# Retention with two mixtures of experts on Trainium2: when the first combinations of tokens run, where the output rows are stored from, and how staged weights are spread

## The chip, the cores and the metric

One NeuronCore of one Trainium2 chip runs the whole program. The metric is device time in microseconds (us); the kernel's time is the median of several executions. The engines are TensorE (PE), VectorE (DVE), ScalarE (ACT), GpSimd (POOL), and SyncE (SP), which here only issues transfers. POOL issues transfers too.

## The reference

Three stages follow one another. Retention, for 4 batches, 8 heads, 576 positions and a head of 64, is attention without softmax, weighted by a decay. Its output, 2304 tokens of width 512, goes into a mixture of 4 experts with given weights, and that into a mixture of 8 experts of which each token uses one.

```
ret = (q k^T / 8) * gamma^(i-j), for i >= j;   x = ret v          # 2304 x 512
p = domain_probs / sum(domain_probs)
out1 = sum over e of p[:, e] * (relu(x w1[e]) w2[e])               # 4 experts, 512 -> 1024 -> 512
e* = argmax(out1 w_gate);  g = softmax(out1 w_gate)[e*];  s = sigmoid(out1 w_output_gate)[e*]
out2 = g * s * (relu(out1 w1s[e*]) w2s[e*])                        # 8 experts, one per token
```

## The kernel before

**Numbers in two parts.** Every fp32 operand of a matmul is split into a high and a low fp16 part (`split`, L163: ACT writes the high part at L164, DVE the low one at L165), and each product is three matmuls.

**Retention** goes in 24 steps of 96 positions. `at_load` (SP) brings q, k and v, `at_split` and `at_a` make scores and the running state (its new value `sn` is made by DVE at L240 and by POOL at L241), and `at_b` (L247) the step's tokens: fp32 `xf`, and their two fp16 parts in the block tile `xc` (ACT L282, POOL L283). `at_store` (L286, SP) writes `xf` to the DRAM tensor `xfd` and finished blocks to `xcd`. Four steps make a block of 384 tokens; there are 6 blocks.

**Mixture 1.** The first expert (e = 0) is interleaved with retention: the loop of L1039 walks experts e, blocks b and units u, and for e = 0 calls `at_hook` (L980), which does one retention step, four times per block. A block of e = 0 has 8 units of the first layer (`l1_first`, matmuls at L431) and three of the second (`l2`, matmuls at L534). Experts 1 to 3 do the first layer by seven products of combinations in place of eight (`l1_mixed`, matmuls at L460), 14 units: m1, m5, m6, m2, m7, m3, m4, each for two halves j. Each of m2, m7, m3 and m4 ends in a `keep` (ACT L418, DVE L419), which stores the hidden layer. m1 ends in a copy on ACT (L484), m6 in an addition on DVE (L494). Three units of `l2` follow, which DVE adds into `acc` (L546).

**Combinations of tokens.** Experts 1 to 3 need sums and differences of token parts, which are the same for each expert. For block b, `x_load` (L296) brings the plain parts from `xcd` into a tile `xc` and, the first time, four pieces of `xfd` into two tiles `xm` (L308). `x_mix` (L312) makes four differences per tile on POOL (L316), `x_keep` (L318) splits the result on ACT (L323) and DVE (L324) into `xc`, and after the second tile POOL stores it to `xcd` for later experts. For block 0 this stands in the last block of e = 0: the load at u = 0 on SP's queue (L1064), the two `x_mix` at u = 3 and 4 (L1071), the two `x_keep` at u = 8 and 9. For the other blocks it stands in e = 1, with the load on POOL's queue.

**Weights of mixture 1.** `w_load` brings eight parts of 512 KB per expert; `w_mixed` (L359) turns them into steps, in which POOL mixes quarters (L372) and ACT and DVE split them. `w_hook` (L1008) does one step. The steps of e = 1 begin in the last block of e = 0.

**Staged weights of mixture 2.** They have to lie in DRAM as two parts, `w1d` and `w2d`, before mixture 2 begins: 64 pieces of 512 KB. `s_hook` (L1015) at its i-th call loads piece i on SP (`s_load`, L556 or L559), issues the store of the split before on SP (L1023), and splits piece i - 2 (`s_split`, L562) into a tile `s16`, of which there are two. Calls stand in the loop at fixed units (L1084):

```python
if e and u in {1: (2, 8, 14) if b else (), 2: (0, 4, 8, 12), 3: (0, 3, 6, 9, 12)}[e]:
    s_hook()
```

**Shared tiles.** The tiles of `w_load`, `s_load` and `xm` come from one pool with tag "wr" and six buffers of 4 KB per partition (L132). The two `xc` buffers are shared by retention's blocks and `x_load`.

**Routing.** In e = 3 each finished `l2` unit puts closures on a list, `gate`, and each unit pops one: `g1` (transpose on PE, L597, split into `xs`), `g2` (gate logits, L608), and per block `g3` (L612), a chain of short DVE operations that ends with the store of three tiles of output rows, 774 KB, to `x1d` on SP's queue (L669). After block 4 `go_early` picks first tokens, whose rows are gathered from `x1d` by POOL (`m_x`, L850). Mixture 2 then works through slots of 128 gathered tokens.

**What sets the order.** Each engine executes its instructions in one order. The framework's planner makes it: it walks the program with times of its own, and an instruction whose operands and buffers it believes ready can move ahead of one that was written earlier. `with tc.issue_after(ins)` adds an edge: what the block writes on the engine of `ins` comes behind `ins`. The dictionary `pace` holds the last `keep` ("act", "dve") and the last weight mix ("pool"), so that splits of staged weights come behind the last `keep` written before them. In e = 1 to 3 no `keep` stands in the `l2` units nor in units 0 to 5, so hooks there hang on the last `keep` of the block before.

Of the kernel before, what the change touches and what calls it, by code (L numbers as in the profile page):

```python
# [104 lines left out]
def kernel(  # L105
# [23 lines left out]
    ht_p = ctx.enter_context(tc.tile_pool(name="ht", bufs=4, side="right"))  # L129
    x_ctx = ExitStack()  # L130
    x_p = x_ctx.enter_context(tc.tile_pool(name="x", bufs=2, side="right"))
    raw_p = ctx.enter_context(tc.tile_pool(name="raw", bufs=6))  # L132
    dram = ctx.enter_context(tc.tile_pool(name="dram", bufs=1, space=DRAM))
    ps = ctx.enter_context(tc.tile_pool(name="ps", bufs=2, space=PSUM))
    w_a = ctx.enter_context(tc.tile_pool(name="w_a", bufs=1))
# [111 lines left out]
    def at_b(s):  # L247
        x2, v2, k2 = spl.pop(s)
        p2 = pm.pop(s)
        c = s % NC  # L250
        o = ps_1.tile([128, KD, C], F32, tag="xo", name="xo")


        def into(r, p, lhsT, rhs, n, last):
            pe.matmul(  # L255
                o[64 * r:64 * r + 64, p], lhsT=lhsT, rhs=rhs,
                start=(p == 0 and n == 0), stop=last, skip_group_check=True,
            )

        for p in range(KD):  # L260
            for n, (x, y) in enumerate(TERMS):
                for r in range(2):
                    into(r, p, v2[:, x, 2 * p + r], p2[:, y, r, p], n, not c and n == 2)
        if c:
            ss = st[s - 1][1]
            for p in range(KD):
                for n, (x, y) in enumerate(TERMS):
                    for r in range(2):
                        row = slice(64 * r, 64 * r + 64)
                        into(r, p, ss[row, x, p], x2[row, y, 0, p], 3 + n, n == 2)  # L270
        st.pop(s - 1, None)
        xf = at_1.tile([128, 2, 2, C], F32, name="xf", bufs=3)
        dve.tensor_tensor(
            out=xf, in0=o.rearrange("p (a k) t -> p a k t", a=2),
            in1=cst("xtab", KD, C).rearrange("p (a k) t -> p a k t", a=2), op=ALU.mult,
        )
        b, r = divmod(s, 4)
        if r == 0:
            xcs[b] = x_p.tile([128, 2, 8, 2, HB], F16, tag="xc", name="xc")
        c, t = 2 * (r // 2), slice(C * (r % 2), C * (r % 2) + C)  # L280
        hi, lo = xcs[b][:, 0, c:c + 2, :, t], xcs[b][:, 1, c:c + 2, :, t]
        act.activation(out=hi, in_=xf, func=ACTF.Copy)  # L282
        pool.tensor_tensor(out=lo, in0=xf, in1=hi, op=ALU.subtract)  # L283
        xfs[s] = xf

    def at_store(s):  # L286
        if s < 0:
            return
        sp.dma_start(out=xfd[s * 128:(s + 1) * 128].rearrange("p (a k) t -> p a k t", a=2), in_=xfs.pop(s))
        b, r = divmod(s, 4)  # L290
        if r == 3:
            dst = xcd[b * 128:(b + 1) * 128]
            sp.dma_start(out=dst[:, :, 0:2], in_=xcs[b][:, :, 0:2])
            sp.dma_start(out=dst[:, :, 3], in_=xcs[b][:, :, 3])

    def x_load(b, mixed, q):  # L296
        t = x_p.tile([128, 2, 8, 2, HB], F16, tag="xc", name="xc")
# [264 lines left out]
    def s_split(i):  # L562
        e, j = divmod(i, 8)
        r = stage.pop(i)
        t = later["pool"].tile([128, 2048], F16, tag="s16", name="s16", bufs=2)
        if j < KD:
            w_parts(r, t.rearrange("p (a f) -> p a f", a=2), None)
            dst = w1d[e * 128:(e + 1) * 128, j].rearrange("p a f -> p (a f)")
        else:
            k = 2 * (j - KD)  # L570
            w_parts(r, t.rearrange("p (k a d) -> p k a d", k=2, a=2), True)
            dst = w2d[e * 128:(e + 1) * 128, k:k + 2].rearrange("p k a d -> p (k a d)")
        return dst, t
# [38 lines left out]
    def g3(b, pl):  # L612
# [53 lines left out]
        dve.scalar_tensor_tensor(  # L666
            out=acc[:, tb, DM], in0=iv[:, 0], scalar=SO2, in1=iv[:, 1], op0=ALU.mult, op1=ALU.mult
        )
        sp.dma_start(out=x1d[t0 * 128:(t0 + TB) * 128].rearrange("(t p) c -> p t c", p=128), in_=acc[:, tb])  # L669

    def unpermute(pl, rr, tiles, n, name):

# [366 lines left out]
    for e in range(E1):  # L1039
        for b in range(NB):  # L1040
            if e == 0:
                units = [] if b == 0 else [lambda b=b, f=f: l1_first(b, f) for f in range(KF)]
                n1 = KF
            else:
                units = l1_mixed(e, b)
                n1 = len(units)
            if (e, b) == (E1 - 1, 0):
                w3_ctx.close()
                open_routing()
            for u in range(n1 + TB):  # L1050
                if u >= n1:
                    l2(e, b, u - n1)
                    if e == E1 - 1:
                        t = b * TB + u - n1
                        gate.append(lambda t=t: g1(t, later["pool"]))
                        gate.append(lambda t=t: g2(t))
                        if u == n1 + TB - 1:
                            gate.append(lambda b=b: g3(b, later["pool"]))
                            if b == NB - 2:
                                gate.append(go_early)  # L1060
                elif units:
                    units[u]()
                if (e, b, u) == (0, NB - 1, 0):
                    x_load(0, False, sp)  # L1064
                if e and u == (2 if (e, b) == (1, 0) else 0) and (e, b) != (E1 - 1, NB - 1):
                    with tc.issue_after(pace["pool"].ins):
                        x_load((b + 1) % NB, e > 1 or b == NB - 1, pool)
                if (e, b) in [(0, NB - 1)] + [(1, i) for i in range(NB - 1)]:
                    for i in range(2):
                        if u == (3 if e == 0 else 6) + i:  # L1070
                            x_mix((b + 1) % NB, i)  # L1071
                        if u == (8, 9)[i] if e == 0 else u == (10, 12)[i]:
                            with tc.issue_after(pace["act"].ins), tc.issue_after(pace["dve"].ins):
                                x_keep((b + 1) % NB, i)
                if e == 0 and u in (2, 5, 8, 9):
                    at_hook()
                if e == 0 and nxt[0] >= NSTEP and b == NB - 1:
                    for _ in range(1 if u < n1 else 3):
                        w_hook(1)
                if e == 1 and b == 0:  # L1080
                    w_hook(1)
                if e and e + 1 < E1 and b >= 1 and u % 3 == 1:
                    w_hook(e + 1)
                if e and u in {1: (2, 8, 14) if b else (), 2: (0, 4, 8, 12), 3: (0, 3, 6, 9, 12)}[e]:  # L1084
                    s_hook()
                if e == E1 - 1:
                    if gate:
                        gate.pop(0)()
                    if b == NB - 1 and u == n1 - 1:
                        while s_at[0] <= n_stage + 2 or pend_store:  # L1090
                            s_hook()
                        m_open()
                        for s in range(EARLY):
                            m_x(s, early[5], s, TE * 128)
# [105 lines left out]
```

## Time and profile before

| | us |
|---|---|
| median of three executions | 1099.57 |
| lowest and highest | 1096.93 and 1101.28 |
| the profiled execution | 1100.34 |
| its span, first to last instruction | 1098.6 |
| PE busy in the span | 1038.0 |
| DVE, ACT, POOL busy | 539.1, 413.6, 283.1 |

The mean granted clock of TensorE is 0.983 of full speed. A busy share is a mean over stages, so the stages have to be read one by one. By the timeline, retention with the first expert takes the first 299 us, experts 1 to 3 of the first mixture end near 866 us, and the second mixture fills the rest. In a timeline row the first number is the start, the second the length, both in us; a row can merge neighbours of one group (x7); what stands in brackets is the idle time of that engine before it and what ended it. A row of busy time by stretch has the stretch, its length, then busy us (and instructions) of PE, weight loads, DVE, ACT and POOL, the granted clock, the DMA share and GB/s.

### The profile page before, as it was taken

To read this page: it belongs to the slowest core of one execution; us is meant where nothing else is said; L and a number is where in the kernel's file an instruction comes from. 1 tells how busy PE (TensorE), PEld (TensorE's weight loads), DVE (VectorE), ACT (ScalarE), POOL (GpSimd) and SP (SyncE) were. 2 spreads that over 40 slices of the span, in tenths; PEclk is the share of its full clock that TensorE was granted. 3 is DMA by queue.
4 is the path that set the end of the run, shared out by engine and by line. 5 is a ranking of instruction groups with operands and counts; after the bars stand their busy time and mean duration, and the time that the engine had idled before them with its cause. 6 is when DMAs were issued, how large, how long until landed. Compare 5 with 4: busy or idle time off the path is not lost.

```text
span 1098.6 us, 24411 instructions
## 1 busy us (share of the span) xinstructions
PE 1038.0 (94%) x10355; PEld 716.1 (65%) x10355; DVE 539.1 (49%) x1037; ACT 413.6 (38%) x821; POOL 283.1 (26%) x292
## 2 busy tenths in 40 slices
PE   4797989999999999999999999988999999999996
PEld 3664555655567777777766666765677577777774
DVE  6873665663836655544655555643665512121211
ACT  5542544542624444333434443432442112121211
POOL 5664555542544442000220000000000021212121
PEclk9898999999999999999999999999999999999998
DMA  9474324301444545655566666546623352491693
GB/s 300 150 216 120 109 89 136 95 31 59 159 154 137 207 172 211 254 195 187 200 223 243 242 242 243 168 156 219 251 107 128 133 217 75 174 356 48 224 385 132
DMA packets 52465, 196.26 MB, mean 179 GB/s; under 512 B 6510, under 2 KB 14334, under 8 KB 50048
## 3 DMA queue, kind: packets, MB, share of 16 engines
q1 hardware_dynamic: 42736, 155.47, 40.1%
q0 software_dynamic: 9616, 39.18, 10.6%
q8 instruction: 83, 1.36, 0.5%
q14 instruction: 30, 0.25, 0.1%
HBM read 184.76 MB, written 56.53 MB: 220 GB/s over the span
## 4 chain that ended last, share of the span: by engine, by line
PE 56%; DMA 16%; issue 11%; DVE 9%; POOL 4%; ACT 2%; POOLq 0%; SPq 0%; DVEq 0%; ACTq 0%
PE po L534 27%; DMA out_dram<-y_s,sidxm 8%; PE ph L460 8%; PE ph L431 7%; PE pq L460 5%; PE py L460 4%; DMA w1d<-s 3%; DVE s L165 2%; DMA wr<-in_w_dram 2%; DVE ht L419 2%; DMA out_dram<-y_s,sidxe 1%; PE xo L255 1%; POOL v L206 1%; POOL vs L199 1%; DMA w2d<-s 1%
## 5 line engine op out<-in xcount | busy, mean ns | idle before, releaser
L534 PE MATMUL po<-w,ht 128*128 128x512 f16 x1728 | 387.3, 383 | 1.3 <-DVE ht L419 1.0
L534 PEld LDWEIGHTS <-ht 128*128 128x128 f16 x1728 | 168.5, 99 | 200.6 <-issue 6.7
L460 PEld LDWEIGHTS <-w 128*128 128x128 f16 x3024 | 249.3, 98 | 4.5
L165 DVE SCALAR_TENSOR_TENSOR s<-sr,s 128x512 f16<-128x512 f32 x128 | 88.6, 730 | 65.8 <-ACT s L164 65.8
L431 PE MATMUL ph<-xc,w 128*128 128x384 f16 (+1 forms) x672 | 104.7, 314 | 17.1 <-ACT xc L282 5.8
L460 PE MATMUL ph<-xc,w 128*128 128x192 f16 x1296 | 119.4, 246 | 0.0
L875 PEld LDWEIGHTS <-lane 128*128 128x128 f16 x1920 | 109.0, 98 | 5.2 <-issue 1.1
L875 PE MATMUL p_h<-x_s,lane 128*128 128x128 f16 x1920 | 111.4, 219 | 0.6 <-issue 0.6
L164 ACT ACTIVATE s<-sr 128x512 f16<-128x512 f32 x128 | 73.4, 625 | 93.1 <-DMA w2d<-s 39.0
L892 PE MATMUL p_y<-lane,h_s 128*128 128x512 f16 x480 | 107.2, 379 | 0.8 <-DVE h_s L885 0.8
L885 DVE SCALAR_TENSOR_TENSOR h_s<-p_h,h_s 128x512 f16<-128x512 f32 x40 | 27.6, 691 | 159.2 <-ACT h_s L884 159.2
L431 PEld LDWEIGHTS <-w 128*128 128x128 f16 x672 | 65.0, 102 | 52.6 <-issue 21.0
L299 POOL DMA_DIRECT2D xc<-xcd x17 | 12.5, 736 | 295.1 <-PE py L460 295.1
L546 DVE SCALAR_TENSOR_TENSOR acc<-po,p_sb,acc 128x512 f32<-128x512 f32 x54 | 40.3, 747 | 97.2 <-PE po L534 97.2
L892 PEld LDWEIGHTS <-h_s 128*128 128x128 f16 x480 | 46.7, 98 | 52.6 <-DVE h_s L885 1.0
L460 PE MATMUL pq<-xc,w 128*128 128x192 f16 x864 | 79.7, 246 | 0.0
L460 PE MATMUL py<-xc,w 128*128 128x192 f16 x864 | 77.2, 246 | 0.0
L165 DVE SCALAR_TENSOR_TENSOR w<-wr,w 128x512 f16<-128x512 f32 x82 | 64.8, 811 | 0.8 <-ACT w L164 0.8
L372 POOL TENSOR_TENSOR wr<-wr 128x512 f32<-128x512 f32 x24 | 36.5, 1523 | 96.3 <-DVE w L165 93.4
L484 ACT ACTIVATE py<-ph 128x384 f32<-128x384 f32 x36 | 17.2, 477 | 107.5 <-PE ph L460 107.1
L895 POOL DMA_INDIRECT out_dram<-y_s,sidxm x17 | 17.3, 1019 | 145.8 <-ACT y_s L894 137.2
L884 ACT ACTIVATE h_s<-p_h 128x512 f16<-128x512 f32 x40 | 23.9, 597 | 79.4 <-PE p_h L875 75.3
(167 smaller groups left out, 1115.4 us busy)
## 6 DMA issues: line engine op xcount, KB each, us to landing
lane<-w1d SPq DMA_DIRECT2D x20, 2048.0 KB
lane<-w2d SPq DMA_DIRECT2D x20, 2048.0 KB
wr<-in_w_dram SPq DMA_DIRECT2D x32, 512.0 KB
sr<-in_w1s_dram SPq DMA_DIRECT2D x32, 512.0 KB
w1d<-s SPq DMA_DIRECT2D x32, 512.0 KB
sr<-in_w2s_dram SPq DMA_DIRECT2D x32, 512.0 KB
w2d<-s SPq DMA_DIRECT2D x32, 512.0 KB
xc<-xcd POOLq DMA_DIRECT2D x12, 960.0 KB, 9.0
```

The lines of the kernel that those rows point to most:

```text
L164: act.activation(out=hi, in_=raw, func=ACTF.Copy, scale=scale)
L165: dve.scalar_tensor_tensor(out=lo, in0=raw, scalar=scale, in1=hi, op0=ALU.mult, op1=ALU.subtract)
L372: pace["pool"] = pool.tensor_tensor(out=quarter(k, to), in0=quarter(k, x), in1=quarter(k, y), op=op)
L419: pace["dve"] = dve.scalar_tensor_tensor(out=dst[1], in0=src, scalar=0.0, in1=dst[0], op0=ALU.max, op1=ALU.subtract)
L431: pe.matmul(ph[:, h0:h1], lhsT=w[:, k, u, f * 128:(f + 1) * 128], rhs=x[:, v, k // 2 + 2 * h0:k // 2 + 2 * h1 - 1:2, k % 2], start=(n == 0 ...
L460: pe.matmul(bank[:, i], lhsT=w[:, k, u, f:f + 128], rhs=x[:, v, d, k], start=(first and i == 0 and n == 0), stop=(n == 5), skip_group_chec ...
L534: pe.matmul(po, lhsT=hts[k // 2][:, x, k % 2, i * 128:(i + 1) * 128], rhs=w[:, k, y], start=(n == 0), stop=(n == 3 * KF - 1),)
L546: dve.scalar_tensor_tensor(out=a, in0=po, scalar=p_sb[:, t, e:e + 1], in1=a, op0=ALU.mult, op1=ALU.add)
L875: pe.matmul(ph[:, j], lhsT=w[:, k, x, f * 128:(f + 1) * 128], rhs=xs[:, y, k], start=(n == 0), stop=(n == 3 * KD - 1),)
L884: act.activation(out=hi, in_=ph, func=ACTF.Relu)
L885: dve.scalar_tensor_tensor(out=lo, in0=ph, scalar=0.0, in1=hi, op0=ALU.max, op1=ALU.subtract)
L892: pe.matmul(po, lhsT=h[:, a, k], rhs=w[:, k, b], start=(n == 0), stop=(n == 3 * KF - 1))
```

## The change

The first `x_load` is tied behind the last retention store on SP, and `x_mix` behind the last POOL work written before it (in retention that is now `at_b`'s subtraction). The store of output rows moves from SP's queue to POOL's. `s16` has three buffers, the shared pool of raw tiles five. Hooks of staged weights: five per block in e = 2 and four in e = 3, where it was four and five; their number stays the same.

```diff
-    raw_p = ctx.enter_context(tc.tile_pool(name="raw", bufs=6))
+    raw_p = ctx.enter_context(tc.tile_pool(name="raw", bufs=5))
...
-        pool.tensor_tensor(out=lo, in0=xf, in1=hi, op=ALU.subtract)
+        pace["pool"] = pool.tensor_tensor(out=lo, in0=xf, in1=hi, op=ALU.subtract)
...
-            sp.dma_start(out=dst[:, :, 3], in_=xcs[b][:, :, 3])
+            pace["sp"] = sp.dma_start(out=dst[:, :, 3], in_=xcs[b][:, :, 3])
...
-        t = later["pool"].tile([128, 2048], F16, tag="s16", name="s16", bufs=2)
+        t = later["pool"].tile([128, 2048], F16, tag="s16", name="s16", bufs=3)
...
-        sp.dma_start(out=x1d[t0 * 128:(t0 + TB) * 128].rearrange("(t p) c -> p t c", p=128), in_=acc[:, tb])
+        pool.dma_start(out=x1d[t0 * 128:(t0 + TB) * 128].rearrange("(t p) c -> p t c", p=128), in_=acc[:, tb])
...
                 if (e, b, u) == (0, NB - 1, 0):
-                    x_load(0, False, sp)
+                    with tc.issue_after(pace["sp"].ins):
+                        x_load(0, False, sp)
...
                         if u == (3 if e == 0 else 6) + i:
-                            x_mix((b + 1) % NB, i)
+                            with tc.issue_after(pace["pool"].ins):
+                                x_mix((b + 1) % NB, i)
...
-                if e and u in {1: (2, 8, 14) if b else (), 2: (0, 4, 8, 12), 3: (0, 3, 6, 9, 12)}[e]:
+                if e and u in {1: (2, 8, 14) if b else (), 2: (0, 3, 7, 10, 14), 3: (0, 4, 8, 12)}[e]:
```

## Rows read from the trace of the kernel before

**Rows 1.** What PE waited for over the whole span (engine, line, releaser: us in total, times, longest)
```profile
PE pg L608 <- DVE xs L165: 9.8, 4, 3.6
```

**Rows 2.** Timeline of POOL, 80 to 100 us (start us, us, instruction, idle before it and releaser)
```profile
88.68 4.47 POOL L316 TENSOR_TENSOR xm<-xm 128x192 f32<-128x192 f32 x7 [4.62 <-DMA xm<-xfd]
...
93.11 0.61 POOL L241 TENSOR_TENSOR sn<-sn,ka 128x256 f32<-128x256 f32 x1
```

**Rows 3.** Timeline of DVE, 80 to 100 us
```profile
84.61 0.41 DVE L240 TENSOR_TENSOR sn<-u,sn 128x256 f32<-128x256 f32 x1
```

**Rows 4.** Timeline of PE, 85 to 110 us
```profile
95.88 0.41 PE L431 MATMUL ph<-xc,w 128*128 128x384 f16 x1 [5.32 <-ACT xc L282]
...
99.14 7.64 PE L431 MATMUL ph<-xc,w 128*128 128x384 f16 x35 [2.84 <-POOL xc L283]
```

**Rows 5.** Chain that ended last, in order of time (start us, us, what)
```profile
143.62 5.85 PE ph L431 x35
```

**Rows 6.** Busy time by stretch: the first five blocks of the last expert of MoE 1
```profile
672.70:709.30 36.60, 34.36 (x292) 23.43 (x291) 19.19 (x55) 13.45 (x29) 1.44 (x2) 0.95 0.56 195
709.30:747.60 38.30, 34.30 (x292) 23.52 (x291) 19.46 (x56) 13.44 (x29) 1.44 (x2) 0.96 0.55 196
747.60:785.00 37.40, 34.29 (x292) 23.39 (x291) 18.91 (x55) 13.26 (x29) 1.44 (x2) 0.95 0.57 200
785.00:820.10 35.10, 32.66 (x292) 22.98 (x291) 20.48 (x57) 13.63 (x30) 0.00 (x0) 1.00 0.47 181
820.10:853.70 33.60, 33.07 (x307) 23.38 (x306) 16.94 (x71) 9.92 (x21) 3.13 (x3) 1.00 0.39 149
```

**Rows 7.** Timeline of ACT, 700 to 720 us
```profile
707.72 1.15 ACT L164 ACTIVATE s<-sr 128x512 f16<-128x512 f32 x2 [1.93 <-DMA w2d<-s]
...
717.23 1.15 ACT L164 ACTIVATE s<-sr 128x512 f16<-128x512 f32 x2 [8.36 <-DMA w2d<-s]
```

**Rows 8.** Timeline of SP's queue, 695 to 720 us
```profile
704.55 0.34 SPq L1023 DMA_DIRECT2D w2d<-s  x1
...
706.69 0.34 SPq L1023 DMA_DIRECT2D w2d<-s  x1
```

**Rows 9.** What SP's queue waited for over the span
```profile
SPq L669 <- DVE ri L643: 84.6, 5, 21.2
```

**Rows 10.** Timeline of POOL, 770 to 890 us
```profile
780.28 0.72 POOL L299 DMA_DIRECT2D xc<-xcd  x1 [35.99 <-PE py L460]
...
880.15 1.00 POOL L851 DMA_INDIRECT x_g<-x1d,gidxm  x1 [26.94 <-DVE sidxm L685]
```

**Rows 11.** Timeline of SP's queue, 860 to 890 us
```profile
872.29 0.39 SPq L669 DMA_DIRECT2D x1d<-acc  x1
```

**Rows 12.** The page's part 6, DMA issues (KB each, median us to landing)
```profile
xc<-xcd POOLq DMA_DIRECT2D x12, 960.0 KB, 9.0
```

**Rows 13.** Groups of instructions by line and form, 270 to 300 us
```profile
L165 DVE SCALAR_TENSOR_TENSOR w<-wr,w 128x512 f16<-128x512 f32 x22 | 19.4, 919 | 0.4 <-ACT w L164 0.4
...
L372 POOL TENSOR_TENSOR wr<-wr 128x512 f32<-128x512 f32 x8 | 12.3, 1536 | 15.4 <-DVE w L165 15.0
...
L324 DVE TENSOR_TENSOR xc<-xm,xc 128x768 f16<-128x768 f32 x2 | 3.0, 1487 | 0.0
```

**Rows 14.** The page's part 5, costliest groups over the span
```profile
L165 DVE SCALAR_TENSOR_TENSOR s<-sr,s 128x512 f16<-128x512 f32 x128 | 88.6, 730 | 65.8 <-ACT s L164 65.8
```

**Rows 15.** Timeline of DVE, 300 to 306 us
```profile
304.19 0.57 DVE L494 TENSOR_TENSOR pq<-ph,s 128x384 f32<-128x384 f32 x1 [4.11 <-PE ph L460]
```

**Rows 16.** Timeline of SP's queue, 262 to 300 us
```profile
281.22 12.15 SPq L348 DMA_DIRECT2D wr<-in_w_dram  x4
```

**Rows 17.** Timeline of PE, 300 to 306 us
```profile
300.97 2.14 PE L460 MATMUL pq<-xc,w 128*128 128x192 f16 x24
```

**Rows 18.** Timeline of ACT, 580 to 600 us
```profile
596.04 0.47 ACT L484 ACTIVATE py<-ph 128x384 f32<-128x384 f32 x1 [3.12 <-PE ph L460]
```

**Rows 19.** Busy time by stretch: third expert of MoE 1
```profile
475.00:652.00 177.00, 176.87 (x1443) 125.37 (x1442) 98.12 (x163) 74.50 (x154) 21.14 (x20) 1.00 0.60 214
```

## The prediction

> **What bounds the kernel now.** I read four views in this order. The page's busy times come first: TensorE (PE) is the bound engine nearly everywhere. Then busy time by stretch: in the third expert of the first mixture PE is busy 176.87 of 177.00 us [rows 19], so nothing can be gained there, only lost. Two stretches are left in which PE waits: retention, and the last expert of the first mixture. Then the list of what PE waited for, then the timelines of the engines that it waited for.
>
> In **retention** POOL is at fault. The first combinations (x_mix of block 0, written in the last block of expert 0) have been moved forward to 88.68 us. POOL sits 4.62 us until their tiles land and runs seven of them, 4.47 us; only then, at 93.11, comes the state step sn that retention needs [rows 2]. Its operand was ready when DVE ended at 84.61 + 0.41 = 85.02 [rows 3]. What hangs on sn comes as late: PE waits 5.32 us, does one matmul, waits 2.84 us more, and does its next 35 matmuls in 7.64 us [rows 4], where the same 35 take 5.85 us elsewhere [rows 5].
>
> In the **last expert** each of four junctions between blocks is stretched. The block-to-block times are 36.60, 38.30, 37.40 and 35.10 us; the fifth junction has no staging left and takes 33.60, with 15 more matmuls [rows 6]. PE waits in four places, 9.8 us in all, for xs, the split of the routing transpose [rows 1], and the granted clock of three of these stretches is 0.95 to 0.96 against 1.00 [rows 6]. xs is late because ACT, in order, is stuck ahead of it: a staged split waits 8.36 us, up to 717.23, for the store that must empty its buffer s16 [rows 7]. That store was issued at 706.69 [rows 8], so it took about 10.5 us; the store issued at 704.55 [rows 8] had landed when the split at 707.72 began [rows 7], after 3.1 us. Three splits hang on the block's last keep and its neighbours, and two buffers make the third of them wait for a slow store.
>
> **The change, part by part.** The sum is made against the profiled execution, 1100.34 us (span 1098.6), which lies 0.8 above the median of the three runs, 1099.57.
>
> *Combinations behind the last retention step.* Out of retention go four tile loads and the two direct loads on SP, POOL's 4.62 us of waiting and eight combinations (seven in 4.47 us, so 0.64 each, 5.1 in all) [rows 2]. sn could start at 85.02 instead of 93.11, 8.1 us earlier, and the eighth combination, behind sn, leaves the chain too: 8.7 us. PE's two waits are 5.32 + 2.84 = 8.16 [rows 4], so both are covered. The slow matmuls give back 7.64 - 5.85 = 1.79. Term: -9.95. Bounds: 0, if another late operand stands at the same place, and -9.95.
>
> In their new place SP's six loads follow the last retention store, where SP has nothing more until 281.22 [rows 16]. With five raw tiles instead of six, four of them held by expert 1's parts, the second pair of combinations has to wait for a freed tile. Today's weight loads show when tiles come free: four issues from 281.22 to 293.37 [rows 16]. From there come 4.62 of landing [rows 2], four combinations, 2.6, the DVE half of x_keep, 1.49 [rows 13], and as much again at most for ACT's half: ready at 291.4 to 303.6. The first product that reads combinations starts at 300.97 [rows 17]. Bounds: 0, and 2.6 late plus a slow stretch of 1.79 as in retention, 4.4. I take 0, since tiles come free in the order in which they were filled, which is the early end.
>
> The eight combinations now also run beside DVE's weight splits. Here 22 splits took 19.4 us beside 12.3 us of POOL mixes [rows 13]; at the 0.73 of a staged split [rows 14] they would take 16.1. So 3.3 was lost to 12.3 of POOL, 0.27 per us, and 5.1 us of combinations cost DVE 1.4. DVE sits idle 4.11 us before 304.19 [rows 15], which covers that: 0. The Trainium skill (SBUF — State Buffer, section SBUF: two separate sides) has GpSimd and a two-input VectorE instruction hold one port pair exclusively, the loser blocked for the whole instruction. By that DVE would lose all 5.1 us, 1.0 past its cover, and the sum would be 1.0 higher; the row shows about a quarter of that loss.
>
> *Third s16 buffer and new hooks.* In the last expert four splits per block replace five; the third of a junction takes the buffer whose store is the early one, as the 3.1 us store was [rows 7, 8], and needn't wait. Without the wait a junction is 33.60 less the PE time of its extra matmuls, 33.07 - 32.66 = 0.41 [rows 6]: 33.19. The four sum to 147.40 [rows 6], so the term is 147.40 - 4 x 33.19 = -14.64. Bounds: 0 (the wait stays), and -14.64.
>
> The third expert takes five splits instead of four per block. ACT sits idle 3.12 us before its first due copy of the next block [rows 18], after its junction's splits; that is the cover, and no transpose or xs stands in a junction there. Bounds 0 and rival D; I take 0.
>
> *Five raw tiles* mean one load fewer ahead of the splits. No row shows a split waiting for its own load. Nearest: 960 KB landed in 9.0 us [rows 12], so 512 KB in an estimated 4.8, less the 3.12 of cover [rows 18] is 1.7 at a junction. Bounds 0 and five junctions of the second expert, 8.4 (three loaders share the tiles only there); I take one, +1.7. At the start one weight load moves behind a split: 0, covered by the part's late use in the second layer, 4.8 if not.
>
> *Output rows' store on POOL.* SP's queue waits 84.6 us for the routing at five of these stores [rows 9], with staged stores and loads queued behind; the move frees them, which is part of the term above. On POOL the six stores wait instead. An issue like this is 0.72 us, and POOL idles 35.99 before the block load [rows 10]; a load for the block after next stands behind, with a block to spare. The last store goes out at 872.29 [rows 11]; landing in 9.0 as POOL's large loads do [rows 12], it would hold the gather at 880.15 [rows 10] to 881.3. Bounds 0 and 1.1; I take 0. The Trainium skill (DMA: Bandwidth & Descriptors, section Issuing engine by pattern) gives plain stores to Sync, and its section Issuing engines are not separate DMA queues says another queue saves only issue time. By that the move wins nothing, and this sum doesn't change; the rows show what the page leaves out, a wait at the head of the queue [rows 9].
>
> Sum: -9.95 - 14.64 + 1.7 = -22.9, so 1077.4. I forecast **1077.5**.
>
> **The rivals.**
> A. The transfers, not the buffers, are late. For: the store of 10.5 us against one of 3.1 [rows 7, 8]. Then the last expert keeps its waits: 1100.34 - 9.95 + 1.7 = 1092.1.
> B. Retention gains nothing, because PE meets another late operand at once: 1100.34 - 14.64 + 1.7 = 1087.4. Against: sn alone held ACT, POOL and PE.
> C. The second combinations come late into expert 1: 1077.4 + 4.4 = 1081.8.
> D. Slower: the stall moves into the third expert. With five splits per block, two of which must get their loads inside the junction, the last split ends late and ACT's first copy of the next block with it. It decides once that split ends over 3.12 us later than now [rows 18]. At the price of the worst junction now, 38.30 - 33.19 = 5.11, six junctions cost 30.7: 1077.4 + 30.7 = 1108.1. Against: PE lost 0.13 us there [rows 19].
> E. It doesn't do what it says: the planner, with ties and buffers changed, puts other work at the same places: about 1100.
>
> **How the numbers follow.** A measurement of this kernel can tell about 0.5%, 5.5 us, from no change. Forecast 0.58 (its own range 1073 to 1083), A 0.10, B 0.08, C 0.06: all are faster by more than that, 0.82. E, and mixtures that end within 5.5 us: 0.10. D: 0.08. The range runs from 1070 (the unknown costs at 0 and some 5 us of replanned order) to 1094, past A; it leaves out D, E and 0.02 below.
>
> **What would show it.** Right: no combination on POOL before the last retention step, PE without the waits near 90 to 99 us; junctions of the last expert near 33.2 us at clock 1.00, no ACT wait over 2 us for a staged store there; x1d on POOL's queue with none of SP's 84.6 us left; the third expert still at 177 us. Wrong: PE waiting for xc in retention for another cause, for xs still, or for py copies in the second or third expert, or at 300.97 for combinations.

## The result and the profile after

The changed kernel takes 1084.3 us (median of four executions, 1082.55 to 1084.66) against 1100.25 for the kernel before beside it (1096.93 to 1101.28): a ratio of 0.9857, 95% interval 0.9833 to 0.9881. The forecast was 1077.5, the range 1070 to 1094. It got faster, as forecast, by 15.9 us in the profiled executions (1100.34 to 1084.43, spans 1098.6 to 1082.7) in place of 22.9.

To see where, I cut both spans at PE's own marks in the timeline: the first matmul of the first expert's last block (the end of retention), the first l2 matmul (L534) of a block in experts 1 to 3, the first matmul of the second mixture, the last matmul.

| stretch | before | after | difference | forecast |
|---|---|---|---|---|
| start to the end of retention | 267.52 | 258.03 | -9.49 | -9.95 |
| from there to the second expert's first l2 ("boundary") | 45.33 | 49.11 | +3.78 | 0 |
| second expert, to the third's first l2 | 177.96 | 177.98 | +0.02 | +1.7 |
| third expert, to the last's first l2 | 176.70 | 181.11 | +4.41 | 0 |
| last expert, four junctions | 147.38 | 131.09 | -16.29 | -14.64 |
| fifth junction and the way to the second mixture | 51.64 | 51.64 | 0 | 0 |
| second mixture, to the last matmul | 223.58 | 223.45 | -0.13 | 0 |
| last matmul to the end of the span | 8.49 | 10.29 | +1.80 | 0 |
| sum | 1098.6 | 1082.7 | -15.9 | -22.9 |

Both gains came, and three small losses stood where the forecast had 0. PE's timeline of the changed kernel shows one gain and two of the losses:

```profile
90.62 0.33 PE L431 MATMUL ph<-xc,w 128*128 128x384 f16 x1
91.43 5.85 PE L431 MATMUL ph<-xc,w 128*128 128x384 f16 x35 [0.49 <-POOL xc L283]
...
286.61 5.34 PE L534 MATMUL po<-w,ht 128*128 128x512 f16 x24 [2.46 <-ACT acc L544]
...
297.25 2.14 PE L460 MATMUL ph<-xc,w 128*128 128x192 f16 x24 [1.01 <-ACT py L484]
...
514.52 1.89 PE L534 MATMUL po<-w,ht 128*128 128x512 f16 x8
517.60 2.76 PE L534 MATMUL po<-w,ht 128*128 128x512 f16 x12 [1.18 <-DVE ht L419]
```

The first two rows answer to [rows 4]: the waits of 5.32 and 2.84 us are 0 and 0.49, and 35 matmuls are back at 5.85; at their end the changed kernel is 9.50 us ahead. The next two are new waits at the boundary, the last one is a new wait in the third expert. POOL's timeline of the changed kernel answers to [rows 2]:

```profile
85.32 0.86 POOL L241 TENSOR_TENSOR sn<-sn,ka 128x256 f32<-128x256 f32 x1 [1.22 <-DVE sn L240]
...
268.18 2.96 POOL L372 TENSOR_TENSOR wr<-wr 128x512 f32<-128x512 f32 x2
274.84 3.85 POOL L316 TENSOR_TENSOR xm<-xm 128x192 f32<-128x192 f32 x4 [3.71 <-DMA xm<-xfd]
278.66 6.66 POOL L372 TENSOR_TENSOR wr<-wr 128x512 f32<-128x512 f32 x4
...
514.42 3.32 POOL L372 TENSOR_TENSOR wr<-wr 128x512 f32<-128x512 f32 x2 [27.38 <-DVE w L165]
```

sn runs at 85.32 in place of 93.11, and the combinations stand behind retention. **Boundary.** The second four of them wait 3.71 us for their tile, and four weight mixes stand behind them. SP's queue says why the tile lands late, and ACT what hangs on that:

```profile
257.02 15.52 SPq L308 DMA_DIRECT2D xm<-xfd  x4
273.64 13.22 SPq L348 DMA_DIRECT2D wr<-in_w_dram  x4
```

```profile
285.36 0.63 ACT L164 ACTIVATE w<-wr 128x512 f16<-128x512 f32 x1 [1.30 <-POOL wr L372]
285.89 0.67 ACT L544 ACTIVATE acc<-po,p_sb 128x512 f32<-128x512 f32 x1
...
294.51 1.15 ACT L164 ACTIVATE w<-wr 128x512 f16<-128x512 f32 x2 [4.83 <-DMA wr<-in_w_dram]
295.57 1.25 ACT L544 ACTIVATE acc<-po,p_sb 128x512 f32<-128x512 f32 x2
```

Four `xm` loads take SP from 257.02 to 272.54, since the last two wait for a raw tile; the last weight load goes out near 286.9. ACT, in order, has weight splits ahead of its copies of the first expert's output (L544): the first copy stands behind a split that waits for POOL's late mixes, the other two behind a split that waits 4.83 us for the last weight part. PE has two `po` buffers and waits for the copies. In the kernel before PE waits nowhere in this stretch, and the same copies stand here:

```profile
292.76 0.67 ACT L544 ACTIVATE acc<-po,p_sb 128x512 f32<-128x512 f32 x1
299.19 1.25 ACT L544 ACTIVATE acc<-po,p_sb 128x512 f32<-128x512 f32 x2
```

Counted from the end of retention, the first copy comes 2.6 us later than before and the other two 5.9.

**Last expert.** Busy time by stretch over its first five blocks, answering to [rows 6]:

```profile
666.23:699.00 32.77, 32.51 (x293) 22.98 (x291) 18.58 (x54) 12.52 (x28) 2.22 (x3) 1.00 0.57 195
699.00:731.77 32.77, 32.52 (x293) 22.96 (x291) 18.58 (x54) 12.52 (x28) 2.23 (x3) 1.00 0.54 195
731.77:764.54 32.77, 32.51 (x293) 22.95 (x291) 18.57 (x54) 12.52 (x28) 2.22 (x3) 1.00 0.54 196
764.54:797.32 32.78, 32.53 (x294) 22.97 (x291) 18.57 (x54) 12.53 (x28) 2.22 (x3) 1.00 0.46 163
797.32:830.90 33.58, 33.05 (x307) 23.34 (x306) 18.74 (x76) 10.86 (x24) 0.77 (x1) 1.00 0.28 99
```

All four junctions are even, at full clock. The wait of [rows 1] is gone. Of the 16.29 us, PE's busy time gave back 135.61 [rows 6] less 130.07, 5.5: matmuls that had run at the lower granted clock. The rest was waiting. One stretch of the kernel before, right behind PE's wait of 3.6 us, shows matmuls at a granted clock of 0.50, which is 1.2 GHz in place of 2.4:

```profile
720.70:724.00 3.30, 3.30 (x12) 1.36 (x10) 0.00 (x0) 0.28 (x1) 0.00 (x0) 0.50 0.74 237
```

**Third expert.** PE's waits in this expert in the changed kernel (us in total, times, longest); the same view of the kernel before lists none:

```profile
PE po L534 <- DVE ht L419: 2.8, 4, 1.2
PE po L534 <- ACT ht L418: 0.7, 1, 0.7
```

DVE's timeline, first at the junction where PE waited 1.18, then at another:

```profile
514.25 2.36 DVE L165 SCALAR_TENSOR_TENSOR s<-sr,s 128x512 f16<-128x512 f32 x2
516.53 0.55 DVE L419 SCALAR_TENSOR_TENSOR ht<-pq,ht 128x384 f16<-128x384 f32 x1
...
545.39 1.28 DVE L165 SCALAR_TENSOR_TENSOR s<-sr,s 128x512 f16<-128x512 f32 x2
```

A staged split stands ahead of a keep whose hidden layer the l2 unit needs, and POOL's mixes at 514.42 stretch it from 1.28 to 2.36. The Trainium skill (SBUF — State Buffer, section SBUF: two separate sides) has the loser of a shared port pair blocked for the other's whole instruction. By that a split would wait, by an estimate from the row, up to 1.66 us, half of POOL's 3.32. The trace agrees in kind: the two splits lost 1.08.

### The profile page after: what moved, and what is told of

It reads as the page before. It is cut to its first block, busy times and chain, and to the rows that moved or that the text cites. A ratio compares the mean times of both kernels' runs of the same rounds, so it can differ in the third digit from the quotient of the medians.

```text
span 1082.7 us, 24429 instructions
## 1 busy us (share of the span) xinstructions
PE 1032.4 (95%) x10355; PEld 713.8 (66%) x10355; DVE 536.4 (50%) x1037; ACT 414.5 (38%) x821; POOL 289.3 (27%) x298
## 4 chain that ended last, share of the span: by engine, by line
PE 45%; issue 11%; DMA 10%; DVE 6%; ACT 1%; POOL 0%; POOLq 0%; SPq 0%; DVEq 0%; ACTq 0%
PE po L534 25%; DMA out_dram<-y_s,sidxm 8%; PE ph L460 8%; PE pq L460 5%; PE py L460 5%; DVE ht L419 2%; DVE s L165 1%; DMA out_dram<-y_s,sidxe 1%; PE tp L597 1%; PE pg L608 1%; DMA w2d<-s 0%; DVE s L505 0%; DVE w L165 0%; PE p_y L892 0%; ACT ht L418 0%
## 5 line engine op out<-in xcount | busy, mean ns | idle before, releaser
L534 PE MATMUL po<-w,ht 128*128 128x512 f16 x1728 | 384.4, 380 | 7.5 <-DVE ht L419 3.9
L534 PEld LDWEIGHTS <-ht 128*128 128x128 f16 x1728 | 167.2, 98 | 205.3 <-DVE ht L419 7.9
L165 DVE SCALAR_TENSOR_TENSOR w<-wr,w 128x512 f16<-128x512 f32 x82 | 61.7, 767 | 10.7 <-ACT w L164 10.6
L164 ACT ACTIVATE w<-wr 128x512 f16<-128x512 f32 x82 | 49.3, 623 | 19.1 <-DMA wr<-in_w_dram 13.0
L895 POOL DMA_INDIRECT out_dram<-y_s,sidxm x17 | 17.3, 1017 | 146.8 <-ACT y_s L894 138.2
```

Of the source, the lines that this page charges most:

```text
L164: act.activation(out=hi, in_=raw, func=ACTF.Copy, scale=scale)
L165: dve.scalar_tensor_tensor(out=lo, in0=raw, scalar=scale, in1=hi, op0=ALU.mult, op1=ALU.subtract)
L534: pe.matmul(po, lhsT=hts[k // 2][:, x, k % 2, i * 128:(i + 1) * 128], rhs=w[:, k, y], start=(n == 0), stop=(n == 3 * KF - 1),)
L895: pool.indirect_dma_start(out=out, out_offset=bass.IndirectOffsetOnAxis(ap=idx[:, s:s + 1], axis=0), in_=y, in_offset=None, bounds_check=N ...
```

## The experiments

Twelve kernels ran in three groups, e1 to e4, e5 to e8 and e9 to e12, once each but for e10 and e12, which ran five times. The totals of a group stand beside its own runs of the kernel before (1098.96, 1095.61 and 1098.59 us). Stretches are compared across groups, since those that an edit doesn't touch agree within 0.2 us, but for three: retention with the ties ended between 256.72 and 259.77 (the changed kernel at 258.03 and 258.39), the boundary with five raw tiles in its first order took between 48.07 and 49.75, and the second mixture, not in the table, took 223.4 to 223.9 us in the result's pair and the first group and 222.7 in the other two. So a single total says little here, and the stretches carry the argument. The last column runs from the start of the program's last store of results (POOL, L895; not the store of output rows to `x1d`) to the end of the span.

| kernel | total | retention ends | boundary | second | third | last, four | last store to end |
|---|---|---|---|---|---|---|---|
| before | | 267.52 | 45.33 | 177.96 | 176.70 | 147.38 | 7.4 |
| changed | 1084.3 | 258.03 | 49.11 | 177.98 | 181.11 | 131.09 | 9.2 |
| e1 no ties | 1093.69 | 266.34 | 49.49 | 177.98 | 181.22 | 131.10 | 9.2 |
| e2 old buffers | 1087.71 | 256.72 | 46.09 | 177.98 | 183.05 | 136.17 | 9.2 |
| e3 old hooks | 1081.65 | 258.30 | 48.99 | 177.98 | 176.69 | 132.07 | 9.2 |
| e4 store on SP | 1085.28 | 259.54 | 49.75 | 177.97 | 181.22 | 131.09 | 7.4 |
| e5 five raw, two s16 | 1087.76 | 257.76 | 48.63 | 177.98 | 181.33 | 135.68 | 9.2 |
| e6 four hooks | 1081.79 | 259.09 | 49.12 | 179.46 | 176.70 | 131.09 | 9.2 |
| e7 hooks moved | 1079.88 | 257.19 | 48.85 | 177.98 | 178.33 | 131.09 | 9.2 |
| e8 boundary | 1080.62 | 258.23 | 45.86 | 177.98 | 181.13 | 131.09 | 9.2 |
| e9 before, store on POOL | 1099.63 | 267.07 | 45.33 | 177.99 | 176.69 | 146.21 | 9.2 |
| e10 combined | 1076.54 | 259.77 | 45.86 | 177.99 | 176.69 | 131.69 | 7.4 |
| e11 combined, one store on POOL | 1076.51 | 259.39 | 45.85 | 177.97 | 176.70 | 131.83 | 7.6 |
| e12 changed, again | 1083.95 | 258.39 | 48.07 | 177.98 | 181.11 | 131.10 | 9.2 |

**e1.** The ties taken out.

```diff
-                    with tc.issue_after(pace["sp"].ins):
-                        x_load(0, False, sp)
+                    x_load(0, False, sp)
...
-                            with tc.issue_after(pace["pool"].ins):
-                                x_mix((b + 1) % NB, i)
+                            x_mix((b + 1) % NB, i)
```

> The changed kernel without its two ties (x_load of block 0, x_mix); everything else stays changed. Stretches of the kernel before and of the changed one: retention's end (start of the 96 first-layer matmuls of expert 0's last block) 267.52 and 258.03 us; from there to the first second-layer matmul of expert 1, the boundary, 45.33 and 49.11. Theory (the ties alone gave retention its 9.5 us, and the combinations, now in the boundary, cost it 3.8): retention's end near 267.5, combinations on POOL before 100 us, boundary near 45.3, whole time near 1090. Rival (the five raw tiles cost the boundary 3.8, not the combinations): boundary stays near 49, whole time near 1094. Rival 2 (five raw tiles alone keep the planner from moving the combinations forward): retention's end stays near 258.

Retention ended at 266.34, 8.3 later than with the ties. POOL's timeline has the old picture, with four combinations ahead of sn instead of seven:

```profile
89.29 2.59 POOL L316 TENSOR_TENSOR xm<-xm 128x192 f32<-128x192 f32 x4 [4.68 <-DMA xm<-xfd]
91.84 0.61 POOL L241 TENSOR_TENSOR sn<-sn,ka 128x256 f32<-128x256 f32 x1
...
283.01 3.85 POOL L316 TENSOR_TENSOR xm<-xm 128x192 f32<-128x192 f32 x4 [6.41 <-DMA xm<-xfd]
```

So the ties make retention's gain. The boundary stayed at 49.49. That rules out the ties and the place of the first four combinations as its cause, but not the second four: with five raw tiles they stand in the boundary here too (last row), and wait 6.41 us for their tile.

**e2.** Six raw tiles, two s16.

```diff
-    raw_p = ctx.enter_context(tc.tile_pool(name="raw", bufs=5))
+    raw_p = ctx.enter_context(tc.tile_pool(name="raw", bufs=6))
...
-        t = later["pool"].tile([128, 2048], F16, tag="s16", name="s16", bufs=3)
+        t = later["pool"].tile([128, 2048], F16, tag="s16", name="s16", bufs=2)
```

> The changed kernel with two s16 and six raw tiles again. The four junctions of the last expert took 147.38 us before and 131.09 changed; the third expert 176.53 and 181.11; the boundary 45.33 and 49.11. Theory (the third buffer removes ACT's wait for the store): the junctions go back to over 140. Rival (four splits in place of five, or the row store's move, removes it): they stay below 134. For the boundary: if five raw tiles make the weights of expert 1 late, it returns to 45 to 46; if the combinations' place does, it stays near 49. For the third expert: if five raw tiles starve it, 176.5; if the fifth split crowds ACT and DVE, it stays near 181 or is worse, since two buffers wait longer.

The boundary fell to 46.09. SP's row in this kernel, against 15.52 us with five tiles:

```profile
255.69 2.02 SPq L308 DMA_DIRECT2D xm<-xfd  x4
```

All eight combinations stand in the boundary here, so their place alone costs at most the 0.8 us that is left over the kernel before.

The last expert's junctions grew by 5.1 only, to 136.17, not back to 147.38.

**e3.** The hooks of before.

```diff
-                if e and u in {1: (2, 8, 14) if b else (), 2: (0, 3, 7, 10, 14), 3: (0, 4, 8, 12)}[e]:
+                if e and u in {1: (2, 8, 14) if b else (), 2: (0, 4, 8, 12), 3: (0, 3, 6, 9, 12)}[e]:
```

> The changed kernel with the old hooks: four splits per block in the third expert, five in the last. Theory (the fifth split, in the first-layer units, crowds the keeps of the third expert): the third expert returns from 181.11 to about 176.5. For the last expert's four junctions (147.38 before, 131.09 changed): if the third buffer is what counts, about 131 to 135; if the fourth hook is, over 140. By the theory of both at once the whole time is near 1081 to 1084; by the rival (hooks needed) near 1090 or more.

The third expert is back at 176.69, and the last expert, with five splits per block again, pays 0.98: 132.07. With three buffers the new hooks cost more than they bring.

**e4.** The store of output rows back on SP's queue.

```diff
-        pool.dma_start(out=x1d[t0 * 128:(t0 + TB) * 128].rearrange("(t p) c -> p t c", p=128), in_=acc[:, tb])
+        sp.dma_start(out=x1d[t0 * 128:(t0 + TB) * 128].rearrange("(t p) c -> p t c", p=128), in_=acc[:, tb])
```

> The changed kernel with the store of output rows on SP's queue again. Theory (its move costs and gives nothing, since the staged splits behind it are not due before the routing ends): within 1.5 us of the changed kernel, junctions of the last expert at 131 to 132, SP's waits for routing back at some 80 us. Rival (SP's wait at the head of its queue held staged stores): ACT waits again for staged stores, and the four junctions take over 135.

No junction moved. The end of the span did: the last store of results starts 7.4 us ahead of it, against 9.2. The total doesn't show it, since retention ended 1.5 later in this execution and the boundary took 0.6 more.

**e5.** e2's second edit alone: five raw tiles, two s16.

```diff
-        t = later["pool"].tile([128, 2048], F16, tag="s16", name="s16", bufs=3)
+        t = later["pool"].tile([128, 2048], F16, tag="s16", name="s16", bufs=2)
```

> The changed kernel with s16 back at two buffers and the five raw tiles kept. Theory: the five raw tiles alone lengthen the stretch between retention and the second expert's first l2 unit (49.11 us in the changed kernel, 46.09 with six raw tiles and two s16), and the third s16 buffer alone shortens the last expert's junctions. Then that stretch stays at 49.1, the four junctions of the last expert take about 136 together (136.17 with both old sizes, 131.09 with both new ones), the third expert about 183 (183.05 and 181.11), and the whole about 1084.4 + 5 + 2 = 1091. Rival: the third s16 buffer, by taking SBUF and shifting the planner's order, is what lengthened the stretch: then it falls to 46 and the whole is about 1088. Second rival: the junctions owe their gain to the five raw tiles: then they stay at 131.

The boundary stayed (48.63) and the junctions went to 135.68: the raw tiles make the one, the third s16 buffer the other. The third expert took 181.33, not the 183 of e2, so two s16 buffers need not cost it anything. What cost e2 1.8 us there stands in e2's own trace, as one wait:

```profile
551.85 1.15 ACT L164 ACTIVATE s<-sr 128x512 f16<-128x512 f32 x2 [6.26 <-DMA w1d<-s]
553.12 0.74 DVE L546 SCALAR_TENSOR_TENSOR acc<-po,p_sb,acc 128x512 f32<-128x512 f32 x1
553.91 2.32 PE L534 MATMUL po<-w,ht 128*128 128x512 f16 x10 [1.78 <-DVE acc L546]
```

A staged split waits for its buffer's store, and DVE's addition into `acc` stands behind it. In e5 a split of the same junction waits 7.32 us, but there the planner put the addition ahead of it. Busy time by stretch at the last expert's junctions in e5, and the wait behind it:

```profile
665.70:699.64 33.94, 32.64 (x294) 22.97 (x292) 18.50 (x54) 12.64 (x28) 2.22 (x3) 1.00 0.54 189
...
733.27:767.69 34.42, 32.64 (x292) 22.96 (x291) 18.49 (x54) 12.64 (x28) 2.22 (x3) 1.00 0.53 187
```

```profile
PE pg L608 <- DVE xs L165: 4.1, 4, 1.5
```

**e6.** Four hooks per block in each of the three experts.

```diff
-                if e and u in {1: (2, 8, 14) if b else (), 2: (0, 3, 7, 10, 14), 3: (0, 4, 8, 12)}[e]:
+                if e and u in {1: (2, 8, 14, 16) if b else (), 2: (0, 4, 8, 12), 3: (0, 4, 8, 12)}[e]:
```

> The changed kernel with four hooks per block in each of the second, third and last expert (the second expert's fourth one in an l2 unit). Theory: the third expert's loss of 4.4 us comes from its five hooks and their places, so with units 0, 4, 8 and 12 it is back at 176.7, the last expert keeps its 131.1, the second expert pays at most 1 us (177.98 now), and the whole is about 1084.4 - 4.4 = 1080. Rival: the third expert lost because of the five raw tiles shared by three loaders; then it stays at 181 and the whole at 1084. Second rival: the second expert, at its limit with weight splits and combinations, loses for the fourth hook what the third gets back (5 blocks by 1 us): about 1084 too, but with 182 in the second expert.

Third expert 176.70, last 131.09, second 179.46: it pays 1.5 for a fourth hook. So four hooks bring the third expert back and cost the last nothing, but the second expert is no free place for them.

**e7.** Five hooks in the third expert at 0, 3, 6, 9, 12.

```diff
-                if e and u in {1: (2, 8, 14) if b else (), 2: (0, 3, 7, 10, 14), 3: (0, 4, 8, 12)}[e]:
+                if e and u in {1: (2, 8, 14) if b else (), 2: (0, 3, 6, 9, 12), 3: (0, 4, 8, 12)}[e]:
```

> The changed kernel with the third expert's five hooks at units 0, 3, 6, 9 and 12 instead of 0, 3, 7, 10 and 14. Theory of places: a hook at unit 7, 10 or 14 hangs on a keep of the same block, so its split stands between the keeps of the last products, and the l2 units wait for late hidden layers; at 0, 3, 6, 9 and 12 (the places that the last expert had before) the third expert takes 176.7 to 178 and the whole about 1081. Theory of the count: five splits per block are what the third expert can't hold beside its weights, wherever they stand: it stays at 180 to 181 and the whole at 1084.

It takes 178.33, between the two theories and nearer to that of places: of the 4.41, the places cost 2.78 and the count 1.63.

**e8.** The boundary's order.

```diff
-                if e == 1 and b == 0:
-                    w_hook(1)
+                if e == 1 and b == 0:
+                    with tc.issue_after(pace["acc"].ins):
+                        w_hook(1)
...
-            act.activation(out=a, in_=po, func=ACTF.Copy, scale=p_sb[:, t, 0:1])
+            pace["acc"] = act.activation(out=a, in_=po, func=ACTF.Copy, scale=p_sb[:, t, 0:1])
...
-                        if u == (3 if e == 0 else 6) + i:
+                        if u == ((3, 10)[i] if e == 0 else 6 + i):
-                        if u == (8, 9)[i] if e == 0 else u == (10, 12)[i]:
+                        if u == (8, 10)[i] if e == 0 else u == (10, 12)[i]:
```

> The changed kernel with the second pair of first combinations written behind all weight mixes of the second expert, and with the weight steps written in the second expert's first block tied behind the last copy of the first expert's output. Theory: PE waits 2.46 and 1.01 us there because ACT's copies of the first expert's output stand behind weight splits, which wait for POOL's mixes (late behind the second combinations, whose tiles land late) and for the last weight part. Then the waits go, the stretch falls from 49.1 to 45.5 to 46.5, and the whole to about 1081. Rival: the second combinations now come too late for the product that reads them, and PE waits there instead: 48 to 52, the whole 1083 to 1087.

The boundary fell to 45.86. PE's timeline in this kernel, where 2.46 stood, and no wait at the later place:

```profile
284.72 5.34 PE L534 MATMUL po<-w,ht 128*128 128x512 f16 x24 [0.37 <-ACT acc L544]
```

The late raw tile is the cause, and the order in which ACT meets it is the price: put in another order, five tiles cost 0.5 us here. The run makes two edits at once, the combinations behind the mixes and the weight steps behind the copies; what each gives isn't shown.

**e9.** The kernel before with the store of output rows on POOL's queue, and nothing else.

```diff
-        sp.dma_start(out=x1d[t0 * 128:(t0 + TB) * 128].rearrange("(t p) c -> p t c", p=128), in_=acc[:, tb])
+        pool.dma_start(out=x1d[t0 * 128:(t0 + TB) * 128].rearrange("(t p) c -> p t c", p=128), in_=acc[:, tb])
```

> The kernel before with one part of the change: the store of output rows on POOL's queue. First theory: the last expert's staged stores are late because SP's queue stands behind the store of output rows (84.6 us of waiting); freed of it, the four junctions, 147.4 us together, fall to about 136, what two s16 buffers and the new hooks give. Rival: the order of the hooks (five splits, three of them at a junction) and the two buffers make the wait, and SP's queue is only a bystander: then the junctions stay at 145 to 148. A second point: from the last store of output to the end of the span the four kernels with this store on POOL's queue take 9.2 us, the two with it on SP's 7.4; if the queue is the cause it is 9.2 here, with nothing else changed.

The junctions stayed: 146.21 for 147.38. One wait of ACT, what PE waited for, and two stretches:

```profile
714.78 1.15 ACT L164 ACTIVATE s<-sr 128x512 f16<-128x512 f32 x2 [8.39 <-issue]
```

```profile
PE pg L608 <- DVE xs L165: 9.0, 4, 3.6
```

```profile
701.63:740.96 39.33, 35.34 (x293) 24.01 (x292) 19.50 (x56) 13.46 (x30) 2.22 (x3) 0.91 0.54 191
740.96:778.44 37.48, 34.32 (x293) 23.36 (x292) 19.48 (x56) 13.44 (x30) 2.21 (x3) 0.95 0.57 197
```

The split waits 8.39 us where it waited 8.36 [rows 7]; the view names no releaser, but the store of its buffer, issued at 704.24, took 10.5 us to land, as long as before. So SP's 84.6 us at L669 [rows 9] were a bystander. The Trainium skill (DMA: Bandwidth & Descriptors, section Issuing engines are not separate DMA queues) says that another issuing engine saves only the time of issuing; the trace agrees, with 1.2 us in four junctions. The longer end came here too, 9.2, and the total, 1099.63, lies among the nine runs of the kernel before beside it (1094.78 to 1101.02).

**e10, e11, e12.** e8's edits, the hooks of before and the store on SP's queue (e10); the same with the first of the six stores on POOL's queue (e11); the changed kernel again, with no edit (e12). Beside the edits of e8, e3 and e4, e11 has:

```diff
-        sp.dma_start(out=x1d[t0 * 128:(t0 + TB) * 128].rearrange("(t p) c -> p t c", p=128), in_=acc[:, tb])
+        (pool if t0 == 0 else sp).dma_start(out=x1d[t0 * 128:(t0 + TB) * 128].rearrange("(t p) c -> p t c", p=128), in_=acc[:, tb])
```

> What the runs so far point to, put together: the changed kernel with the hooks of the kernel before (four per block in the third expert, five in the last), the store of output rows back on SP's queue, the second pair of first combinations written behind the weight mixes and the weight steps of the second expert's first block tied behind the last copy of the first expert's output. If the parts add: boundary 46, third expert 176.7, last expert 132.1, end 1.8 us shorter: 3.2 + 4.4 - 1.0 + 1.8 = 8.4 us under the changed kernel, about 1076, a ratio to before of 0.977 to 0.980. If the store on SP's queue with five hooks per block brings the late stores back, the last expert takes 134 to 140 and the whole 1078 to 1084.

> The combined kernel with only the first of the six stores of output rows on POOL's queue, five on SP's. If the longer end belongs to any use of POOL's queue for this store, the stretch from the last store of output to the end of the span is 9.2 us; if it grows with each store, 7.7; if only the late ones count, 7.4.

> The changed kernel once more, on the same chip and beside the same runs of before as the combined kernel, so that the two can be told apart: 0.9857 of before within 0.003 by the first measurement, and if the parts add, 8 us above the combined kernel.

The combined kernel takes 1076.54 (five executions, 1074.55 to 1077.45), a ratio of 0.9801, interval 0.9779 to 0.9823; the changed kernel on the same chip 1083.95, 0.9869, 0.9848 to 0.9890. The intervals lie apart: the combined kernel beats both. In the two profiles, e10 and e12, the parts add up to 7.8 us of the 8.4 that were expected; retention, which ended 1.4 later in e10, takes that to 6.4.

From the start of the last store of results to the end it is 7.4 us in e10, with no store of output rows on POOL's queue, 7.6 in e11 with one, and 9.2 with six. Most of the difference lies in one operation, POOL's long drain at the program's closing line, the largest of three (duration in ns: least, median, largest; then the first and last start). It stands here in the kernel before, in e11 and in the changed kernel, with none, one and six stores:

```profile
L1196 POOLq DRAIN  x3: 46/107/2766, 1095.0 to 1098.3; - x3
```

```profile
L1199 POOLq DRAIN  x3: 46/107/3011, 1070.9 to 1074.5; - x3
```

```profile
L1198 POOLq DRAIN  x3: 46/107/4072, 1077.8 to 1082.4; - x3
```

One store adds 0.25 us to it, six add 1.31, some 0.22 each. That rules out that any use of the queue costs all of it, and that only late stores count: e11's is the first of the six. It grows with each store. What POOL does in the drain isn't shown.

## Why the prediction was right, and where its terms were off

1. **Retention**, -9.95, measured -9.49. Right in mechanism and size; in these two executions PE's new wait of 0.49 us for POOL's part of xc is the difference, and e1 shows that the ties make the gain. Other executions with the ties ended retention up to 1.7 us later and 1.3 earlier. Rival B falls.
2. **Junctions**, -14.64, measured -16.29. The step that was off is the 33.19 of a free junction, taken from the fifth: with the wait gone a junction takes 32.77. Rival A falls, though its premise holds: in the changed kernel three stores issued from 701.28 to 704.15 still land 7.8 to 9.3 us later, but with a third buffer no split of the last expert waits for one.
3. The reason given for it was partly wrong. "The third of a junction ... needn't wait" holds with four splits and with five (e3: 132.07). But the third buffer and new hooks each take most of the wait alone (e3 saves 15.3; the hooks with two buffers and the store on POOL's queue save 11.2 to 11.7, e2 and e5), so they overlap. And "the move frees them, which is part of the term above" fell in e9: the store's move took 1.2 of 16.3.
4. **Five raw tiles**, +1.7 at a junction of the second expert: nothing was lost there (+0.02). The loss came at the start, where two steps failed that were taken at 0: "At the start one weight load moves behind a split", and the late second combinations, which the working followed to the product that reads them and not to the weight mixes behind them on POOL. Measured +3.78, inside its bound of 4.8 and near rival C's 4.4, but by another way: PE never waited for combinations or for the late part itself; what had no cover were ACT's copies of the first expert's output, behind the splits that wait. e2 beside e5 lays it on the raw tiles, e8 on the order.
5. **Third expert**, forecast 0, measured +4.41. "That is the cover" looked at ACT's first copy of the next block; the place that decides is the last keeps of the same block, on DVE and ACT. Rival D had the stretch right and the place wrong; its price of 5.11 per junction was 0.7 as a mean of six. e7 parts it into places and count.
6. **Store on POOL's queue**, 0 with a bound of 1.1, measured +1.80, outside the bound and at the end of the program, where the working did not look; e4 and e9 show it from both sides, and e11 that it grows with each store. The landing in 9.0 us that the bound took was high as well: the six stores landed in 4.0 to 5.7.

The errors, 0.46 - 1.65 - 1.7 + 3.78 + 4.41 + 1.80 and 0.1 of other stretches the other way, make the 7.0 us by which the gain fell short.

The measured time lies above the forecast's own range, 1073 to 1083, and inside the stated one only because that reached to 1094 for rival A, which didn't come. So the direction and the two gains were foreseen, but the three losses were not, and it is luck that the wide end of the range had room for them. One of its signs of being wrong did show, a wait of PE for a `py` copy in the second expert, 1.01 us, and one of its signs of being right failed: the third expert took 181 us, not 177.

## What to carry to other kernels

When a change takes a buffer from a shared pool, list every user of the pool in order and ask, on each engine, what stands behind the first instruction that now waits: here it was the output copies of the expert before. A split that is tied behind one keep can still stand ahead of the next ones, so write such filler behind the last result that PE is about to read, or far from it. And try remedies for one wait one at a time: the third buffer with the old hooks and the old queue would have done (e10: 131.69), while the new hooks beside it cost 3.4 us net (4.4 less 1.0) and the store's move 1.8. Three s16 buffers beside six raw tiles were not run.

## What the runs showed that was not expected

Output-row stores on POOL's queue lengthen the program's end: the stretch from the start of the last store of results to the end of the span is 7.4 us in three kernels without them, 7.6 in one with one and 9.2 in ten with six, whatever else they change. POOL's drain there takes 2.77, 3.01 and 4.07 us. And the price of a junction's wait was not its length alone: with waits of up to 1.5 us (e5) PE was busy 32.64 us in a stretch at a granted clock of 1.00; in e9, where the longest was 3.6, it was busy 34.32 and 35.34 at 0.95 and 0.91.
